# Sixteen-by-sixteen diagonal blocks moved as one strided piece a lane, in a linear-attention and two-layer MLP kernel on one core

## The chip, the cores and the metric

The kernel runs on one core of one Trainium2 chip. The metric is the device time of one execution in microseconds (us); a kernel's time is the median over its runs.

## What is computed

The reference has three parts. The first is a recurrence over 768 positions for 4 x 8 heads, with a 40 x 40 state a head:

```python
for t in range(S):
    y[:, :, t] = np.einsum('bhd,bhde->bhe', rt, state)
    Sa = np.einsum('bhde,bhe->bhd', state, at)
    state_decay = state * wt[:, :, None, :] - np.einsum('bhd,bhe->bhde', Sa, bt)
    state = state_decay + np.einsum('bhd,bhe->bhde', vt, kt)
```

Its output, as 3072 rows of 320, goes through a gated layer (sigmoid(x @ w_gate) * (x @ w_val), 1536 wide, then w_out) and through a second layer (the maximum of three products, 768 wide, then w_out). All is f32.

## The kernel before

**Tiling.** The recurrence is worked in chunks of 64 positions. An "item" is two chunks of four pairs of heads; there are 24 items, in 12 pairs. Inside a chunk the recurrence is a triangular system, so each chunk needs the inverse of a 64 x 64 unit triangle. It is built from 16 x 16 diagonal inverses, which are joined to 32 x 32 (`join`) and to 64 x 64 (`merge`) by small matmuls. The two MLP layers run as f32 products split into high and low parts; their first products (`wave`, L923 to L953) fill TensorE between the small matmuls of the recurrence, and after some 600 us only MLP work is left.

**The way of the diagonal blocks.** For each pair of items `prep` forms the triangles N on VectorE (L438) and writes their 32 x 32 diagonal blocks to the DRAM tensor d1 (L449, eight DMAs). Each 32 x 32 block is one row of 4 KB in d1. `tri` (L479) then does the following.
- Two DMAs (L487) bring the two 16 x 16 diagonal sub-blocks of every 32 x 32 block back, one on each half of the 128 lanes, into the tile T.
- 28 small operations (L497 add, L499 multiply) invert all 128 blocks at once by substitution, on VectorE for the first two pairs and on GpSimd for the other ten; a memset (L505) sets the ones on the diagonal.
- ScalarE copies T transposed into the tile Tt (L506).
- Two DMAs (L510) write Tt into the diagonal places of the DRAM tensor d2, whose other places were set to zero once (L356).

`spread` reads d2 by four DMAs into the tile E (L522), in another arrangement of lanes, and VectorE transposes E (L525). `join` follows (matmuls L543 and L554), then `merge` (L576, L587), `ga` (L605) and the four `step`s that carry the state (L633, L651, L665, L689).

**What sets the order.** Every operation is a task with a duration, reads and writes. A planner (`Plan.play`) plays them through a model of the engines and writes out one fixed order for each engine; the tile framework then puts in the semaphore waits. All data DMAs are issued by SyncE, whose queue SP is in order: a DMA that must wait holds up all that stands behind it. Behind L522 on SP stand the loads of the next items (`ew`, L381 and L382 or L384; 836 KB each) and of `vr` (L624) and `vk` (L627). VectorE and GpSimd are in order too.

**Places.** The tiles share areas of SBUF: T0 and T1 (two slots of T, 128 x 16 x 16) lie in the area F1 (F in the profile), Tt in B3 (B in the profile). The planner also has a rule that could add filler matmuls (`fill`), with its level at 0.0, at which it adds none.

Of the kernel before, what the change touches and what calls it, by code (L numbers as in the profile page):

```python
# [9 lines left out]
BF16 = mybir.dt.bfloat16  # L10
# [5 lines left out]
B, H, S, D = 4, 8, 768, 40  # L16
NTOK, DM = B * S, H * D
C = 64
NP = 4
# [11 lines left out]
            F1=["N0", "N1", "N2", "N3", "DC", "T0", "T1", "Y2"], F2=["MA0", "MA1", "MA2", "MA3", "TD0"],  # L31
            B3=["E0", "E1", "YM0", "Tt", "tmpPOOL"], B4=[f"KH{k}" for k in range(6)],
# [46 lines left out]
class Task:  # L79
    def __init__(self, eng, dur, fn, name):  # L80
        self.eng, self.dur, self.fn, self.name = eng, dur, fn, name
        self.before, self.after, self.users = set(), set(), []
        self.filler, self.fills, self.late = False, 0, 0.0
        self.lat, self.goal, self.due, self.banks, self.keep, self.nbytes = 0.0, 1e9, 1e9, [], None, 0


class Plan:
# [10 lines left out]
    SPARE, AHEAD, MORE = 0.7, 7.0, 1  # L98
    FILL, LEVEL = 0.23, 0.0
    HOLD, BY = 0.4, 40.0  # L100

    def __init__(self):
        self.tasks, self.wrote, self.readers = [], {}, {}
        self.warm = False
        self.stage = None
# [36 lines left out]
    def play(self):  # L142
# [18 lines left out]
        pe_end, done_work = 0.0, []  # L161
# [8 lines left out]
        while len(order) < len(self.tasks):  # L170
            for e, q in ready.items():
# [4 lines left out]
                while q:  # L176
# [5 lines left out]
                    if (t.rank <= hold + self.BY or t.dur < self.HOLD) and all(reader.get(p, (e, 0))[0] == e or reader[p][1] <= now + 1e-9 for p in t.of) and (  # L182
# [5 lines left out]
                        if e == "PE" and t.filler:  # L188
                            self.fill(t, now, pe_end, done_work, clock)
                        if e == "PE":  # L190
                            now_ = now + t.late
                        t.start = now
                        t.end = free_at[e] = clock.run(now_, t.dur, t.name) if e == "PE" else now + t.dur
# [5 lines left out]
                        if e == "PE":  # L199
                            pe_end = t.end  # L200
                            done_work.append((now_, t.end, Clock.WORK.get(t.name, 0.94) * t.dur))
                            credit = credit - t.dur if t.thin else min(self.DENSE, credit + t.dur)
# [33 lines left out]
    def fill(self, t, now, before, work, clock):  # L236


        end = now + t.dur
        lo = end - Clock.TICK  # L240
        while work and work[0][1] < lo - 4 * Clock.TICK:
            work.pop(0)
        got = t.dur * Clock.WORK.get(t.name, 0.94)
        for a, b, w in work:
            if b > lo:
                got += w * (b - max(a, lo)) / (b - a)
        one = self.FILL / (1.0 if clock.warm else 0.51)
        idle = min(self.SPARE * max(0.0, now - before), self.AHEAD)
        n = max(0, math.ceil((self.LEVEL - got) / (0.9 * self.FILL)))
        n = max(min(n, int(idle / one) + self.MORE), int(idle / one) if n else 0)  # L250
        if not n:
            return
        t.fills = n
        at = max(before, now - n * one)
        stop = clock.run(at, n * self.FILL, "fill")
        work.append((at, stop, 0.9 * n * self.FILL))
        t.late = max(0.0, stop - now)

    def emit(self):
        for t in self.play():  # L260
            if t.fills:
                self.filled(t)
            if t.fn:
                t.fn()


class Attn:
# [6 lines left out]
    def open(self, mem, ps):  # L274
# [3 lines left out]
                      ST=[L, NP, D], ew=[L, EWW], AB=[L, NU, C], SW=[L, NP, D], T=[128, 16, 16], Tt=[128, 16, 16], DC=[128, 2 * NU, C], Y2=[128, 2 * NU, 16],  # L278
# [22 lines left out]
        self.pl.filled = self.filled  # L301
# [30 lines left out]
    def pe(self, dur, fn, reads, room, name, keep, n=1):  # L332
        t = self.pl.add("PE", dur, fn, reads, (), name, psum=keep, room=room, n=n)
        t.filler = self.pl.warm and name != "x"
        return t

    def filled(self, t):

        x = self.c.bitcast(BF16)
        for n in range(t.fills):  # L340
            self.nc.tensor.matmul(self.ps[t.banks[0]], x[:, 0:128], x[:, 128:640], start=True, stop=True)


    def begin(self):
# [13 lines left out]
        self.pl.add("POOL", 0.3, lambda: nc.gpsimd.memset(self.tY[0], 0.0), (), ["tY"], "z")  # L358
        for k in range(B):
            for j in range(2):  # L360
                self.pl.add("POOL", 0.18, lambda k=k, j=j: nc.gpsimd.memset(self.SW[k][j], 0.0), (), [("SW", k, j)], "z")
# [117 lines left out]
    def tri(self, i0, slot):  # L479
# [4 lines left out]
        d1 = self.d1[k // 2].rearrange("h t y (a b) -> (h t y) a b", b=32)  # L484
        for h in range(2):
            p, s = slice(64 * h, 64 * h + 64), slice(16 * h, 16 * h + 16)
            self.load(lambda p=p, s=s: nc.sync.dma_start(out=T[p], in_=d1[:, s, s]),  # L487
# [17 lines left out]
        self.pl.add("POOL", 0.15, lambda: nc.gpsimd.memset(T.rearrange("p i j -> p (i j)")[:, 0:256:17], 1.0), (), tT, "one")  # L505
        self.act(570, lambda: nc.scalar.copy(self.Tt, T.rearrange("p i j -> p j i")), tT, ["Tt"], "Tt")  # L506
        q = 32 * (i0 % 4)
        for h in range(2):
            p, s = slice(64 * h, 64 * h + 64), slice(16 * h, 16 * h + 16)
            self.load(lambda p=p, s=s: nc.sync.dma_start(out=self.d2[q:q + 64, s, s], in_=self.Tt[p]), ["Tt", ("d2", k // 2)],  # L510
# [204 lines left out]
    def add(self):  # L715
        self.begin()
        self.pl.warm = True
# [723 lines left out]
```

## Time and profile before

| | us |
|---|---|
| median of 3 runs | 1149.53 |
| lowest and highest run | 1143.75, 1161.09 |
| the profiled execution, its own time | 1145.82 |
| its span, first to last instruction | 1143.9 |
| TensorE matmuls busy | 1057.4 (92% of the span) |
| VectorE, ScalarE, GpSimd busy | 655.4, 498.8, 384.9 |

The profile is one execution. PE is the matmul queue of TensorE, PEld its weight loads, SPq the time that SyncE's queue needs to issue a DMA. A row of the timeline gives the start, the duration, the engine, the line, the tiles and, in brackets, how long the engine had stood idle and what ended that. The chain of waits is followed back from the last instruction, at each step to what released it.

### The profile page before, as it was taken

What the parts mean: (1) busy time and instruction counts of PE and PEld (TensorE: products, weight loads), DVE (VectorE), ACT (ScalarE), POOL (GpSimd) and SP (SyncE); (2) the same over time, 40 slices, a digit from 0 to 9 for tenths busy, and PEclk for the clock granted to TensorE, in tenths of its full rate; (3) what the DMA queues carried; (4) which work ended last, traced back from release to release, by engine and by line L of the source; (5) the groups of instructions that cost most, each with busy time, mean ns of one, the idle gap of its engine ahead of it and who ended that gap; (6) DMA issues with size and microseconds to landing.
All of it is one profiled execution on the core that took longest, in us unless ns stands there. A gap on an engine that the chain in (4) does not pass through costs nothing.

```text
span 1143.9 us, 28812 instructions
## 1 busy us (share of the span) xinstructions
PE 1057.4 (92%) x11954; PEld 887.2 (78%) x11954; DVE 655.4 (57%) x1144; ACT 498.8 (44%) x1091; POOL 384.9 (34%) x551
## 2 busy tenths in 40 slices
PE   5389889999999999998889999999999999999997
PEld 4388677787888787786677778888888888888886
DVE  7679647677668586659873792492493222222122
ACT  2166456576656575667543443353323122122111
POOL 1024523244234344333354553353322222122110
PEclk9995759898978998968879999999999999999999
DMA  6736545475475565554540623333232011000000
GB/s 160 169 97 156 105 94 108 99 168 123 85 170 114 112 151 109 132 160 142 176 152 10 199 71 111 111 107 111 85 117 91 11 51 51 1 33 17 8 23 26
DMA packets 190159, 114.85 MB, mean 100 GB/s; under 512 B 123158, under 2 KB 166806, under 8 KB 188150
## 3 DMA queue, kind: packets, MB, share of 16 engines
q1 hardware_dynamic: 190022, 112.94, 38.5%
q8 instruction: 96, 1.57, 0.6%
q14 instruction: 41, 0.34, 0.1%
HBM read 87.21 MB, written 25.69 MB: 99 GB/s over the span
## 4 chain that ended last, share of the span: by engine, by line
PE 75%; DVE 10%; DMA 5%; issue 4%; ACT 2%; SPq 2%; POOL 1%; DVEq 0%; POOLq 0%; ACTq 0%
PE ps L902 39%; PE ps L972 6%; PE ps L1042 5%; PE ps L605 3%; PE ps L651 3%; PE ps L689 3%; PE ps L665 3%; PE ps L945 3%; DMA D<-ew 2%; PE ps L554 2%; PE ps L633 1%; DMA Q<-ew 1%; PE ps L543 1%; PE ps L468 1%; PE ps L576 1%
## 5 line engine op out<-in xcount | busy, mean ns | idle before, releaser
L748 POOL TENSOR_TENSOR C<-C,C 128x512 fp32r<-128x512 f32 x76 | 102.3, 1347 | 323.4 <-ACT C L911 319.3
L902 PE MATMUL ps<-Q,B 128*128 128x512 f32 x768 | 182.7, 390 | 0.0
L902 PEld LDWEIGHTS ps<-Q,B 128*128 128x128 f32 x768 | 143.0, 188 | 28.5
L911 ACT CAST C<-C 128x512 fp32r<-128x512 f32 x108 | 67.1, 621 | 224.3 <-DVE C L1056 138.5
L1056 DVE TENSOR_TENSOR C<-ps,C 128x512 f32<-128x512 f32 x72 | 49.8, 692 | 189.9 <-PE ps L902 189.9
L902 PE MATMUL ps<-Q,D 128*128 128x512 f32 x480 | 115.7, 393 | 0.0
L902 PE MATMUL ps<-Q,A 128*128 128x512 f32 x384 | 111.6, 444 | 0.0
L925 DVE TENSOR_TENSOR C<-ps,C 128x512 f32<-128x512 f32 x72 | 49.6, 689 | 105.2 <-PE ps L902 100.3
L902 PEld LDWEIGHTS ps<-Q,D 128*128 128x128 f32 x480 | 90.8, 190 | 19.1 <-issue 0.3
L902 PEld LDWEIGHTS ps<-Q,A 128*128 128x128 f32 x384 | 79.1, 213 | 18.8 <-issue 0.6
L902 PE MATMUL ps<-Q,F 128*128 128x512 f32 x384 | 92.2, 389 | 0.0
L707 POOL TENSOR_TENSOR R<-B 104x256 f32<-104x256 f32 x48 | 44.3, 923 | 140.4 <-DVE B L705 138.9
L902 PEld LDWEIGHTS ps<-Q,F 128*128 128x128 f32 x384 | 72.1, 188 | 15.0
L923 ACT ACTIVATE C<-ps 128x512 f32<-128x512 f32 x72 | 42.9, 597 | 81.3 <-PE ps L902 75.8
L499 POOL TENSOR_TENSOR B<-F 128x14 f32<-128x14 f32 (+6 forms) x140 | 47.2, 337 | 76.0 <-DMA F<-d 66.5
L1042 PE MATMUL ps<-R,C 128*128 128x320 f32 x432 | 69.1, 309 | 0.2 <-DVE C L748 0.2
L1042 PEld LDWEIGHTS ps<-R,C 128*128 128x128 f32 x432 | 66.1, 188 | 3.2 <-DVE C L748 0.4
L689 PE MATMUL ps<-Q,B 128*64 128x104 f32 (+1 forms) x768 | 55.7, 288 | 7.8 <-ACT Q L676 3.5
L672 DVE TENSOR_TENSOR Q<-ps,R 64x256 f32<-64x256 f32 x96 | 40.6, 423 | 34.4 <-PE ps L665 24.5
L689 PEld LDWEIGHTS ps<-Q,B 128*64 128x64 f32 (+1 forms) x768 | 43.2, 144 | 18.3 <-DVE Q L672 5.3
L665 PE MATMUL ps<-Q,Q 104*64 104x104 f32 x768 | 54.7, 292 | 1.5 <-ACT Q L654 1.5
L497 POOL TENSOR_TENSOR F<-F,B 128x14 f32<-128x14 f32 (+6 forms) x140 | 51.0, 364 | 10.3
(162 smaller groups left out, 1948.9 us busy)
## 6 DMA issues: line engine op xcount, KB each, us to landing
D<-ew SPq DMA_DIRECT2D x18, 835.7 KB
part<-C SPq DMA_DIRECT2D x30, 256.0 KB
Q<-part SPq DMA_DIRECT2D x30, 256.0 KB
D<-in SPq DMA_DIRECT2D x14, 512.0 KB
Q<-vr SPq DMA_DIRECT2D x32, 208.0 KB
x<-Q SPq DMA_DIRECT2D x18, 256.0 KB
Q<-x SPq DMA_DIRECT2D x18, 256.0 KB
R<-vk SPq DMA_DIRECT2D x48, 80.0 KB
```

Source lines behind the costliest of these rows:

```text
L497: e.tensor_tensor(out=T[:, j + 1:16, 0:j], in0=T[:, j + 1:16, 0:j], in1=t, op=ALU.add)
L499: e.tensor_tensor(out=t, in0=T[:, j + 1:16, j:j + 1].to_broadcast([128, k, j]), in1=T[:, j:j + 1, 0:j].to_broadcast([128, k, j]), op=ALU.mult)
L665: nc.tensor.matmul(ps[64 * x:64 * x + 64, n, 0:L], GA[:, x * NP + n], X[:, x * NP + n], start=True, stop=True)
L689: nc.tensor.matmul(ps[64 * x:64 * x + m, n, 0:L], KH[:, h * D:h * D + m], Z[:, h], start=True, stop=True)
L707: self.pool(256, lambda: nc.gpsimd.tensor_tensor(out=Y, in0=tY, in1=P, op=ALU.mult), ["tY", ("P", i % NB["P"])], [("Y", s % NB["Y"])], "Y")
L748: eng.tensor_tensor(out=out, in0=a, in1=hi.bitcast(F32), op=ALU.subtract)
L902: nc.tensor.matmul(self.bank(t), a[:, c], b, start=n == 0, stop=n == len(ops) - 1)
L911: self.act(NT, lambda: nc.scalar.copy(hi(), h()), [th], [t1], "hi")
L925: self.dve(NT, lambda: nc.vector.tensor_tensor(out=sg(), in0=self.bank(t2), in1=sg(), op=ALU.mult), [tsg], [tsg], "gate", of=t2)
L972: nc.tensor.matmul(self.bank(a, m), u[:, c], v(), start=f == f0 and n == 0, stop=f == 11 and n == 2)
L1042: nc.tensor.matmul(self.bank(a, k)[:, 0:DM], u()[:, c], v, start=f == 0 and n == 0, stop=f == 5 and n == 2)
L1056: self.dve(NT, lambda t=t, h=h: nc.vector.tensor_tensor(out=h(), in0=self.bank(t), in1=h(), op=ALU.max), [th], [th], "max", of=t)
```

## The change

T and Tt become 128 x 16 x 32, so that each lane holds 16 rows with a pitch of 32 elements, as the 32 x 32 blocks in d1 and d2 have. A transfer then takes 496 consecutive elements (1984 B) of a lane, from the first element of a diagonal sub-block to its last, where before it took 16 rows of 16 elements (64 B). Between the rows lie 16 elements that do not belong to the sub-block: coming in, they are what d1 holds there and are not used; going out, they are zeros, for which Tt is set to zero once at the start by a new memset on GpSimd. They fall on places of d2 that are zero. The transfers of a pair stay four, to the same lanes, and L449, L522 and all later steps are as before. T1 moves from the area F1 to B3. The filler rule is taken out of the planner; the order that it writes out holds the same matmuls. In the diff, lines of the new kernel stand 45 or so lower in number.

```diff
-            F1=["N0", "N1", "N2", "N3", "DC", "T0", "T1", "Y2"], F2=["MA0", "MA1", "MA2", "MA3", "TD0"],
-            B3=["E0", "E1", "YM0", "Tt", "tmpPOOL"], B4=[f"KH{k}" for k in range(6)],
+            F1=["N0", "N1", "N2", "N3", "DC", "T0", "Y2"], F2=["MA0", "MA1", "MA2", "MA3", "TD0"],
+            B3=["E0", "E1", "YM0", "Tt", "T1", "tmpPOOL"], B4=[f"KH{k}" for k in range(6)],
...
-    SPARE, AHEAD, MORE = 0.7, 7.0, 1
-    FILL, LEVEL = 0.23, 0.0
...
-T=[128, 16, 16], Tt=[128, 16, 16]
+T=[128, 16, 32], Tt=[128, 16, 32]
...
         self.pl.add("POOL", 0.3, lambda: nc.gpsimd.memset(self.tY[0], 0.0), (), ["tY"], "z")
+        self.pl.add("POOL", 0.3, lambda: nc.gpsimd.memset(self.Tt, 0.0), (), ["Tt"], "z")
...
-        d1 = self.d1[k // 2].rearrange("h t y (a b) -> (h t y) a b", b=32)
+        d1 = self.d1[k // 2].rearrange("h t y a -> (h t y) a")
+        flat, Tt = (x.rearrange("p i j -> p (i j)")[:, 0:496] for x in (T, self.Tt))
         for h in range(2):
-            p, s = slice(64 * h, 64 * h + 64), slice(16 * h, 16 * h + 16)
-            self.load(lambda p=p, s=s: nc.sync.dma_start(out=T[p], in_=d1[:, s, s]),
+            p, s = slice(64 * h, 64 * h + 64), slice(528 * h, 528 * h + 496)
+            self.load(lambda p=p, s=s: nc.sync.dma_start(out=flat[p], in_=d1[:, s]),
...
-        self.pl.add("POOL", 0.15, lambda: nc.gpsimd.memset(T.rearrange("p i j -> p (i j)")[:, 0:256:17], 1.0), (), tT, "one")
-        self.act(570, lambda: nc.scalar.copy(self.Tt, T.rearrange("p i j -> p j i")), tT, ["Tt"], "Tt")
+        self.pl.add("POOL", 0.15, lambda: nc.gpsimd.memset(flat[:, 0:496:33], 1.0), (), tT, "one")
+        self.act(570, lambda: nc.scalar.copy(self.Tt[:, :, 0:16], T[:, :, 0:16].rearrange("p i j -> p j i")), tT, ["Tt"], "Tt")
...
-            p, s = slice(64 * h, 64 * h + 64), slice(16 * h, 16 * h + 16)
-            self.load(lambda p=p, s=s: nc.sync.dma_start(out=self.d2[q:q + 64, s, s], in_=self.Tt[p]), ["Tt", ("d2", k // 2)],
+            p, s = slice(64 * h, 64 * h + 64), slice(528 * h, 528 * h + 496)
+            self.load(lambda p=p, s=s: nc.sync.dma_start(out=self.d2[q:q + 64].rearrange("b i j -> b (i j)")[:, s], in_=Tt[p]), ["Tt", ("d2", k // 2)],
```

SP's queue at the start, from the second block's return (L487, `tri2`) over the first block's way out (L510, `tri0`) to its spread (L522), before:

```order
L624 DMA Q_99<-vr 104x4x128
L624 DMA Q_98<-vr 104x4x128
L487 DMA F_90<-d_57 64x16x16
L510 DMA d_58<-B_92 64x16x16 x2
L487 DMA F_90<-d_57 64x16x16
L627 DMA R_96<-vk 64x320
L522 DMA B_92<-d_58 32x16x32 x4
```

The same place of the changed kernel, where L443, L466 and L478 are the old L487, L510 and L522:

```order
L580 DMA Q_99<-vr 104x4x128
L580 DMA Q_98<-vr 104x4x128
L443 DMA B_92<-d_57 64x496
L466 DMA d_58<-B_92 64x496 x2
L443 DMA B_92<-d_57 64x496
L583 DMA R_96<-vk 64x320
L478 DMA B_92<-d_58 32x16x32 x4
```

No instruction has moved; four transfers have another form, and T1 is now named by the area B. The same holds over the whole queue.

GpSimd's first memsets of tiles, before (B_92 is the area with E, R_95 holds the states, B_94 the tile tY):

```order
L354 MEMSET B_92 128x1024
L361 MEMSET R_95 104x160 x2
L358 MEMSET B_94 104x256
L354 MEMSET B_92 128x1024
L361 MEMSET R_95 104x160 x6
```

The same place of the changed kernel:

```order
L308 MEMSET B_92 128x1024
L313 MEMSET B_92 128x512
L316 MEMSET R_95 104x160 x2
L312 MEMSET B_94 104x256
L308 MEMSET B_92 128x1024
L316 MEMSET R_95 104x160 x6
```

One memset, that of Tt, has come in second, ahead of those of the states. TensorE's, VectorE's and ScalarE's orders hold the same instructions at the same places.

## Rows read from the trace of the kernel before

**Rows 1.** The page: the chain that ended last, by engine.
```profile
PE 75%; DVE 10%; DMA 5%; issue 4%; ACT 2%; SPq 2%; POOL 1%; DVEq 0%; POOLq 0%; ACTq 0%
```

**Rows 2.** Windows: stretch, length, busy of PE, PEld, DVE, ACT, POOL, clock, DMA share, GB/s.
```profile
60.00:540.00 480.00, 446.78 (x8589) 374.91 (x8584) 343.09 (x634) 295.41 (x706) 183.23 (x376) 0.85 0.54 125
540.00:1143.90 603.90, 581.32 (x2842) 487.81 (x2842) 270.62 (x407) 189.41 (x351) 197.75 (x158) 0.97 0.24 75
```

**Rows 3.** Waits: who waited for whom, us in total, times, longest.
```profile
POOL B L499 <- DMA F<-d: 66.5, 10, 13.7
DVE F L525 <- DMA B<-d: 15.9, 5, 8.4
PE ps L543 <- DMA B<-d: 9.2, 4, 7.1
```

**Rows 4.** Issues on SP by line: ns shortest, median and longest.
```profile
L487 SPq DMA_DIRECT2D F<-d x24: 600/661/1302, 24.5 to 466.6; - x24
L510 SPq DMA_DIRECT2D d<-B x24: 601/656/1679, 38.6 to 486.3; - x24
L356 SPq DMA_DIRECT2D d<-B x1: 357/357/357, 6.2 to 6.2; - x1
...
L627 SPq DMA_DIRECT2D R<-vk x48: 484/518/4800, 30.7 to 566.9; - x48
```

**Rows 5.** Timeline 24 to 45 us, the first two blocks.
```profile
38.63 1.64 SPq L510 DMA_DIRECT2D d<-B  x2
40.32 0.67 SPq L487 DMA_DIRECT2D F<-d  x1
...
42.71 1.91 SPq L522 DMA_DIRECT2D B<-d  x4
...
44.79 0.26 PE L543 MATMUL ps<-B,F 32*32 32x16 f32 x2 [7.09 <-DMA B<-d]
```

**Rows 6.** Timeline 387 to 390 us: a load of vk and its reader.
```profile
387.55 0.51 SPq L627 DMA_DIRECT2D R<-vk  x1
...
389.99 0.72 ACT L628 COPY Q<-R 64x640 f32<-64x640 f32 x1 [0.20 <-DMA R<-vk]
```

**Rows 7.** Timeline 128 to 144 us, the third block's way out and the fourth's return.
```profile
128.86 1.36 SPq L510 DMA_DIRECT2D d<-B  x2
130.31 1.98 SPq L487 DMA_DIRECT2D F<-d  x2
132.38 1.39 SPq L624 DMA_DIRECT2D Q<-vr  x1
133.87 2.17 SPq L522 DMA_DIRECT2D B<-d  x4
...
138.42 1.25 DVE L525 STREAM_TRANSPOSE F<-B 128x1024 f32<-128x1024 f32 x1 [1.93 <-DMA B<-d]
```

**Rows 8.** The chain of waits, pieces: start, us, what.
```profile
212.21 3.15 DMA B<-d
...
307.16 3.73 DMA F<-d
318.43 7.02 DMA D<-ew
...
387.01 2.30 DMA B<-d
```

**Rows 9.** Groups by line and form: busy us, mean ns, idle before.
```profile
L499 POOL TENSOR_TENSOR B<-F 128x56 f32<-128x56 f32 x20 | 9.0, 449 | 1.5
...
L497 POOL TENSOR_TENSOR F<-F,B 128x56 f32<-128x56 f32 x20 | 7.9, 396 | 1.4
```

**Rows 10.** Timeline 0 to 11 us: the first memset, the first matmuls.
```profile
0.74 0.95 POOL L354 MEMSET B<- 128x1024 f32 x1 [0.29 <-POOLq L1431]
...
4.53 1.18 PEld L633 LDWEIGHTS ps<-R 104*40 104x40 f32 x8 [4.53 <-POOL R L361]
...
10.99 1.65 PE L468 MATMUL ps<-R,D 104*128 104x104 f32 x8 [4.88 <-DVE D L410]
```

More of the change, by code (lines that the diff above doesn't have):

```diff
@@ L1 @@
-import math
 from contextlib import ExitStack
@@ L9 @@
 F32R = mybir.dt.float32r
-BF16 = mybir.dt.bfloat16
 AF = mybir.ActivationFunctionType
@@ L82, in __init__ @@
         self.before, self.after, self.users = set(), set(), []
-        self.filler, self.fills, self.late = False, 0, 0.0
         self.lat, self.goal, self.due, self.banks, self.keep, self.nbytes = 0.0, 1e9, 1e9, [], None, 0
@@ L103, in __init__ @@
         self.tasks, self.wrote, self.readers = [], {}, {}
-        self.warm = False
         self.stage = None
@@ L160, in play @@
         now, seq, credit = 0.0, 0, self.DENSE
-        pe_end, done_work = 0.0, []
         clock = Clock()
@@ L187, in play @@
                             t.banks, banks[:] = banks[:t.n], banks[t.n:]
[L188 to L191, printed above, removed]
                         t.start = now
-                        t.end = free_at[e] = clock.run(now_, t.dur, t.name) if e == "PE" else now + t.dur
+                        t.end = free_at[e] = clock.run(now, t.dur, t.name) if e == "PE" else now + t.dur
                         done = t.end + max(t.lat, self.LAT[1] * any(b.eng == "PE" for b in t.before))
@@ L199, in play @@
                         if e == "PE":
-                            pe_end = t.end
-                            done_work.append((now_, t.end, Clock.WORK.get(t.name, 0.94) * t.dur))
                             credit = credit - t.dur if t.thin else min(self.DENSE, credit + t.dur)
@@ L234, in play @@
         return order
[L236 to L257, printed above, removed]
     def emit(self):
         for t in self.play():
-            if t.fills:
-                self.filled(t)
             if t.fn:
@@ L277, in open @@
                       GA=[L, 2 * NU, C], XZ=[128, 2, 2 * NP, L], VR=[L, NP, 168], Y=[L, NP, C], tY=[L, NP, C],
-                      ST=[L, NP, D], ew=[L, EWW], AB=[L, NU, C], SW=[L, NP, D], T=[128, 16, 16], Tt=[128, 16, 16], DC=[128, 2 * NU, C], Y2=[128, 2 * NU, 16],
+                      ST=[L, NP, D], ew=[L, EWW], AB=[L, NU, C], SW=[L, NP, D], T=[128, 16, 32], Tt=[128, 16, 32], DC=[128, 2 * NU, C], Y2=[128, 2 * NU, 16],
                       E=[128, 2 * NU, C], TD=[128, 2 * NU, 32], YM=[128, 2 * NU, 32], tmpPOOL=[128, 64],
@@ L333, in pe @@
         t = self.pl.add("PE", dur, fn, reads, (), name, psum=keep, room=room, n=n)
-        t.filler = self.pl.warm and name != "x"
         return t
[L337 to L341, printed above, removed]
     def begin(self):
@@ L716, in add @@
         self.begin()
-        self.pl.warm = True
         for i in range(4):
```

1 line of the change is left out of this document (removed).

## The prediction

> **What bounds the kernel now.** I read the chain by engine first: TensorE holds 75% of it, DMA 5%, SP's issuing 2% [rows 1]. The windows come next. From 540 us to the end only MLP work is left and PE is busy for 581 of 604 us; nothing of the change reaches that far, so what it can win or lose it does before 540. From 60 to 540 us PE is busy for 446.8 of 480 us at a mean granted clock of 0.85, so 33.2 us are idle, and half the full clock was granted for 0.15 x 480 / 0.5 = 144 us of the stretch [rows 2]. Those 33.2 us and the start's idle time are all that shorter waits could give back directly. Third, the waits on the transfers that change. GpSimd waits 66.5 us in total for the returning blocks (F<-d), but it is not the engine the end hangs on. The spread (B<-d) is waited for by the matmuls of L543 for 9.2 us, of which one wait is 7.1 us, and by VectorE's transpose L525 for 15.9 us in five waits [rows 3]. The one of 7.1 us is at the start, where PE stands idle until 44.79 [rows 5]. So the blocks' way through DRAM counts at the start and where VectorE, in order, stands at L525.
>
> **What the change removes.** 48 transfers (24 in, 24 out) each go from 1024 pieces of 64 B to 64 pieces of 1984 B. Each costs two things: the issue on SP and the time to landing. The issue takes 661 ns (L487) and 656 ns (L510) in the median. A transfer of 64 lanes with one piece each stands in the trace: vk, 1280 B a lane, takes 518 ns; L356, one piece of 4 KB on each of 128 lanes, took 357 ns [rows 4]. I take 0.52 us, the nearest row, which saves 0.14 us an issue; the bounds are nothing and 0.30. As to landing, the second L510 of the start's pair begins at 38.63 + 0.71 = 39.34 (half of the 1.64 us is the pair's other issue, with a gap) and L522, which waits for it, begins at 42.71, so 3.37 us from issue to use [rows 5]. The chain has 3.73 us for a returning block [rows 8]. A load of vk is used 389.99 - 387.55 = 2.44 us after its issue began [rows 6]. I take 2.44 us for the new transfers, since it is the nearest row in shape and size; the bounds are 2.44 and 3.37, and a loss only if the bytes count (a rival below).
>
> Here the Trainium skill has a rule that speaks against the change. Its page "DMA: Bandwidth & Descriptors", section "Anatomy of one DMA", fits a DMA as about 2.0 us fixed plus its bytes over 436 GB/s, with no term for the number of pieces; the fit is for the other way of issuing, from GpSimd. By it a transfer of 124 KB in place of 64 KB lands 0.14 us later, not earlier. The rows agree with it as to the fixed part (2.44 us for 80 KB) but not as to the 64 KB transfers, which take 3.4 to 3.7 us.
>
> **The sum, place by place.**
> - The start. L510's pair is issued by SP in 2 x 0.52 + 0.05, the second beginning at about 39.1 instead of 39.34, counting the L487 ahead of it too; it lands by 41.5, so L522 moves from 42.71 to 41.5. SP is free by then, as L487 (40.32) and L627 behind it are also earlier. PE waits for nothing else at 44.79. Gain 1.2 us, bounds 0.4 and 1.5. To the first block's return, further ahead, I give nothing, as ScalarE's copy, which L510 waits for, stands in its queue behind the copies of the first steps; if it counted it would be 3.37 - 2.44 = 0.9 more.
> - 128.86 to 133.87 us. SP runs L510 twice, L487 twice and a load of vr, and reaches L522 with no wait for the landing [rows 7]. The four issues take 3.43 us with gaps; at 0.52 and a gap of 0.05 each they take 2.28. The load of vr behind them took 1.39 us and I give it 0.9, since the four before it leave 256 pieces where 4096 were queued. L522 is then 1.7 us earlier, of which VectorE's wait at L525 can use 1.93 [rows 7]. Gain 1.7, bounds 0.3 and 1.9.
> - The spreads that land in the chain's pieces of 212.21 and 387.01 [rows 8]: there too SP goes from the issues of the blocks to L522 with no wait for a landing, and each saves 0.14, two ahead of the one, four ahead of the other. Gain 0.8 together, bounds 0 and 1.8 (at 0.30 an issue).
> - 307 us: GpSimd gets its block 3.73 us after the second issue, on the chain; at 2.44 that is 1.3 us less. The next piece of the chain is a load of ew issued at 318.43 [rows 8], which is released through GpSimd's work, so it moves along. Gain 1.3, bounds 0 and 1.5.
> - The other seven of the twelve blocks: PE's waits at L543 are but for tenths all at the start, and L525 waits in five places only [rows 3]. Gain 0, hidden by the other work of PE and VectorE; if that cover were gone each would give up to 2 x 0.9 us.
>
> Together 5.0 us less, of 33 + 7 us of idle time that could be had; bounds 0.7 and 6.7 from these places alone.
>
> **What it adds.** One memset of 128 x 512 on GpSimd, half of the 0.95 us that 128 x 1024 took; behind it are the memsets of the states, which PE's first matmuls wait for at 4.53. These move to about 5.0, and PE's next work begins at 10.99 on VectorE's result [rows 10]: hidden, 0, at most 0.5. The 28 small operations and the copy keep their element counts, and only the pitch of their rows doubles. No row shows that pitch; the nearest are two forms of 56 elements, of which one writes packed rows and the other rows of T, 449 and 396 ns [rows 9]. The difference of 53 ns as a bound of either sign makes 29 x 0.053 = 1.5 us a block, which counts in the first two blocks, where VectorE does them: 3 us either way; I take 0, as the form that writes into T is no dearer. 48 x 60 KB = 2.9 MB more are moved, over DMA engines that are busy for 0.54 of the time [rows 2]: 0 here, priced below. No wait is added, and the filler's removal removes no instruction.
>
> The sum for the profiled execution is 1145.8 - 5.0 = 1140.8 us (its span is 1.9 us shorter than its time, and all terms lie inside the span). The median of the three runs is 3.7 us above that execution, and the runs are 17 us apart. A new median should lie between the two bases, 1140.8 and 1144.5; I predict 1143 us.
>
> **Rivals.**
> - Hidden anyway: in the steady part another input is late as soon as the block is earlier (a load of ew, a step of the recurrence, PE itself). For it: PE is 93% busy there; the chain has little DMA. Against: the start has no such cover. It leaves those 1.2 us: 1148 us.
> - The bytes count, slower than before. At 125 GB/s, the rate of the stretch [rows 2], a block's 4 x 60 KB more take 2.0 us of the DMA engines. A load of ew queued behind a block's transfers would land that much later, and VectorE, which waits for it, with it. The chain's piece at 318.43 is such a load [rows 8]; taken for three of the blocks it makes 3 x 2.0 = 6 us, less the 1.2 of the start: 1149.5 + 4.8 = 1154 us. It decides if a lane's piece of 2 KB holds an engine longer than its 16 pieces did; a vk of 80 KB used after 2.44 us speaks against.
> - The clock turns. 144 us of the stretch are at 1.2 GHz [rows 2], and which parts these are hangs on how PE's thin matmuls and gaps fall. If earlier blocks close gaps and a fifth of that time goes to 2.4 GHz, it saves 144 x 0.2 x 0.5 = 14 us: about 1130 us. The same the other way gives 1157 us, slower than before; its point of decision is about 10 us more at 1.2 GHz, which takes the 5 us of the forecast.
> - SP is the real limit: the longest issue of a vk load took 4.8 us against 0.52 [rows 4], and it stood right behind an L510 pair. If the small pieces in the rings were the cause, 4.3 us of SP's time come free there and a like amount in the other long issues. The chain gives SP only 2% [rows 1], so the forecast counts none of it; if two such places counted it would be 1143 - 8.6 = 1134 us.
>
> **Chances.** Forecast 0.42; hidden 0.20; bytes 0.08; clock better 0.10, clock worse 0.10; SP 0.10. Range 1129 to 1158, which takes in both clock cases and the spread of the runs. A change of 2% (23 us) is about what a measurement of this kernel can tell from none: faster than 1126.5 needs the better clock and SP together, 0.07; slower than 1172.5 needs twice the worse clock, 0.03; within, 0.90.
>
> **What would show it.** In the profile of the changed kernel: L443 and L466 issue in about 0.5 us; the first L543 begins near 43.5 us instead of 44.79, and the first waiting GpSimd or VectorE row after a return is 2.4 to 2.9 us behind its issue; L478 after the third block comes 1.7 us sooner behind its L466; VectorE's wait for B<-d falls from 15.9 us to about 11; no SP issue behind an L466 pair takes over 2 us. I am wrong if landings stay at 3.3 us or more, if VectorE's waits for ew grow, or if the granted clock from 60 to 540 us leaves 0.82 to 0.88.

## The result, and the profile after

The changed kernel is on record with 1157.01 us in the median of 20 executions (1144.58 to 1162.92), the kernel before with 1151.88 (1141.38 to 1161.70, also 20). The ratio is 1.0068 with a 95% interval of 1.0039 to 1.0097. This is inside the forecast range and inside 2%, but the kernel looks slower where 5.0 us less, and a median of 1143, were forecast. The ratio, here and in the experiments, is taken from the executions that lie no more than 1.5% above the fastest of their own kernel, which here are 18 of the changed kernel and 13 of the kernel before. The means of those are 1156.1 and 1148.3 us; the means of all 20 and 20 are 1156.8 and 1152.6, a difference of 4.2 +- 3.6 us (as everywhere below, the interval is of 95%). So almost half of the 0.68% comes from which executions are counted: the kernel before has the fastest one (1141.38), and for that its seven longest drop out. The profiled execution of the changed kernel took 1144.58 us (span 1142.7), 1.2 us less than that of the kernel before, not 5.0.

One observation has to come first, since the rest of the ratio can't be read without it. Some executions take about 1146 us and others about 1157, at nearly the same granted clock. For the executions of the kernel before that others are compared with, which it is goes by the place of the execution among the others, as the lists further down show. The profiled execution is mostly one of the shorter ones (16 of the 20 that were taken are under 1150 us). On record 10 of 20 executions of the kernel before were under 1150 us, and one of 20 of the changed kernel, the profiled one. The experiments below look for how much of the difference this makes.

The page of the changed kernel, engines, chain and DMA totals:

```profile
PE 1056.2 (92%) x11954; PEld 886.6 (78%) x11954; DVE 654.9 (57%) x1144; ACT 498.4 (44%) x1091; POOL 389.2 (34%) x552
...
DMA packets 144079, 117.79 MB, mean 103 GB/s; under 512 B 74006, under 2 KB 120726, under 8 KB 142070
...
PE 74%; DVE 10%; DMA 6%; issue 4%; ACT 2%; POOL 1%; SPq 1%; DVEq 0%; POOLq 0%; ACTq 0%
```

The chain differs from [rows 1] by one per cent each in PE, DMA and SP, too little to read from one execution. The DMA totals of the kernel before were these:

```profile
DMA packets 190159, 114.85 MB, mean 100 GB/s; under 512 B 123158, under 2 KB 166806, under 8 KB 188150
```

That is 46080 fewer packets now and 2.9 MB more, which is the change (48 x 960, 48 x 60 KB). The windows of the changed kernel, with the columns of [rows 2]:

```profile
60.00:540.00 480.00, 444.82 (x8572) 373.52 (x8570) 343.24 (x630) 294.86 (x707) 186.78 (x376) 0.86 0.52 131
540.00:1142.70 602.70, 581.35 (x2842) 487.83 (x2842) 269.24 (x405) 189.24 (x351) 198.01 (x158) 0.98 0.24 74
```

PE's busy time, its clock and what follows 540 us are what they were. The DMA engines are busy for 0.52 in place of 0.54 although they move more. The waits that answer to [rows 3], and VectorE's for ew, first the one of the kernel before and then those of the changed kernel:

```profile
DVE D L400 <- DMA D<-ew: 23.9, 11, 5.0
```

```profile
POOL B L455 <- DMA B<-d: 38.8, 5, 10.6
...
POOL B L455 <- DMA F<-d: 22.3, 4, 12.1
DVE D L355 <- DMA D<-ew: 21.1, 14, 4.4
...
DVE F L481 <- DMA B<-d: 13.9, 4, 7.6
...
PE ps L499 <- DMA B<-d: 10.6, 5, 7.0
```

The buffer of T moved, so half of the returns are now named B<-d. VectorE's wait for the spread fell from 15.9 to 13.9 us, its wait for ew from 23.9 to 21.1; PE's did not fall in this execution (9.2 to 10.6). The issues on SP, to be held against [rows 4] (ns shortest, median, longest):

```profile
L443 SPq DMA_DIRECT2D F<-d x12: 481/578/759, 24.4 to 430.6; - x12
L443 SPq DMA_DIRECT2D B<-d x12: 462/568/600, 37.6 to 464.4; - x12
...
L466 SPq DMA_DIRECT2D d<-B x24: 472/584/1394, 38.1 to 484.5; - x24
...
L583 SPq DMA_DIRECT2D R<-vk x48: 470/512/1288, 30.5 to 565.8; - x48
```

The issue of a changed transfer fell by 0.08 us, not by the 0.14 that the forecast took. The longest issue of a vk load fell from 4800 to 1288 ns. The timeline of the start and of the third block, as [rows 5] and [rows 7]:

```profile
38.14 1.22 SPq L466 DMA_DIRECT2D d<-B  x2
39.40 0.60 SPq L443 DMA_DIRECT2D B<-d  x1
...
42.35 1.91 SPq L478 DMA_DIRECT2D B<-d  x4
...
44.33 0.26 PE L499 MATMUL ps<-B,F 32*32 32x16 f32 x2 [6.99 <-DMA B<-d]
...
127.24 1.13 SPq L466 DMA_DIRECT2D d<-B  x2
128.47 1.19 SPq L443 DMA_DIRECT2D B<-d  x2
129.75 2.10 SPq L580 DMA_DIRECT2D Q<-vr  x1
132.70 1.91 SPq L478 DMA_DIRECT2D B<-d  x4
...
136.60 1.25 DVE L481 STREAM_TRANSPOSE F<-B 128x1024 f32<-128x1024 f32 x1 [2.82 <-DMA B<-d]
```

At the start the spread issue comes 0.36 us earlier and PE 0.46; from the second way-out issue (38.14 + 0.61 = 38.75) to L478 it is 3.60 us, more than the 3.37 of before. In the third block the four issues take 2.42 us from the first of L466 to the end of L443, near the forecast (2.28), but the load of vr behind them took 2.10 us where 0.9 was forecast, and L478 came 5.46 us behind its first L466, not 3.3.

### The profile page after: what moved, and what is told of

It is laid out like the page before. It is cut to its first block, busy times and chain, and to the rows that moved or that the text cites. A ratio compares the mean times of both kernels' runs of the same rounds, so it can differ in the third digit from the quotient of the medians.

```text
span 1142.7 us, 28813 instructions
## 1 busy us (share of the span) xinstructions
PE 1056.2 (92%) x11954; PEld 886.6 (78%) x11954; DVE 654.9 (57%) x1144; ACT 498.4 (44%) x1091; POOL 389.2 (34%) x552
## 4 chain that ended last, share of the span: by engine, by line
PE 74%; DVE 10%; DMA 6%; issue 4%; ACT 2%; POOL 1%; SPq 1%; DVEq 0%; POOLq 0%; ACTq 0%
PE ps L857 39%; PE ps L927 6%; PE ps L997 5%; PE ps L561 3%; PE ps L607 3%; PE ps L621 3%; DMA D<-ew 3%; PE ps L900 3%; PE ps L645 3%; PE ps L510 2%; PE ps L423 1%; PE ps L532 1%; PE ps L589 1%; PE ps L929 1%; PE ps L928 1%
## 5 line engine op out<-in xcount | busy, mean ns | idle before, releaser
L857 PEld LDWEIGHTS ps<-Q,A 128*128 128x128 f32 x384 | 78.3, 211 | 18.4 <-issue 0.6
L621 PEld LDWEIGHTS ps<-Q,Q 104*64 104x64 f32 x768 | 45.6, 164 | 11.0 <-issue 6.7
L703 POOL TENSOR_TENSOR Q<-Q,Q 128x512 fp32r<-128x512 f32 x33 | 46.0, 1411 | 18.2 <-ACT Q L842 18.2
```

The costliest lines, as they stand in the source:

```text
L621: nc.tensor.matmul(ps[64 * x:64 * x + 64, n, 0:L], GA[:, x * NP + n], X[:, x * NP + n], start=True, stop=True)
L703: eng.tensor_tensor(out=out, in0=a, in1=hi.bitcast(F32), op=ALU.subtract)
L857: nc.tensor.matmul(self.bank(t), a[:, c], b, start=n == 0, stop=n == len(ops) - 1)
```

## The experiments

Each run has 12 executions of its own, and its ratio is to executions of the kernel before that were taken in the same set (35 of them, or 17 where a kernel stands alone). Kernels of one set ran on the same chip. For each run the mean of all 12 executions is given too, since the two lengths of execution make a median jump. Such a mean is known to some 3.5 us. The changed kernel is the base of all edits.

**First set: both kernels, and the transfers put back.** The first run, e1_before, is the kernel before without an edit, and e2_after the changed kernel without an edit. e3_layout puts both transfers back to sixteen rows of 64 B and keeps all else of the change:

```diff
+        dn = self.d1[k // 2].rearrange("h t y (a b) -> (h t y) a b", b=32)
...
-            self.load(lambda p=p, s=s: nc.sync.dma_start(out=flat[p], in_=d1[:, s]),
+            self.load(lambda p=p, s=s: nc.sync.dma_start(out=T[p][:, :, 0:16], in_=dn[:, (s.start // 528) * 16:(s.start // 528) * 16 + 16, (s.start // 528) * 16:(s.start // 528) * 16 + 16]),
...
-            self.load(lambda p=p, s=s: nc.sync.dma_start(out=self.d2[q:q + 64].rearrange("b i j -> b (i j)")[:, s], in_=Tt[p]), ["Tt", ("d2", k // 2)],
+            self.load(lambda p=p, s=s: nc.sync.dma_start(out=self.d2[q:q + 64, 16 * (s.start // 528):16 * (s.start // 528) + 16, 16 * (s.start // 528):16 * (s.start // 528) + 16], in_=self.Tt[p][:, :, 0:16]), ["Tt", ("d2", k // 2)],
```

Here `s.start // 528` is the half, 0 or 1.

e4_in does only the second of these two replacements, so that the way in stays in one piece and the way out is in rows.

e1_before. 

> The kernel before against itself, for the spread of the comparison and for the trace of another execution. All theories: ratio 1.000, interval no wider than 0.6% to each side. If executions differ by some ten us from one to the next in one place (theory M: the program has several courses, and a change only shifts how often each is taken), this trace and that of the next run, laid beside those in hand, show the place: one stretch of 20 to 100 us in which the distance of like matmuls grows by 8 us or more.

e2_after. 

> The changed kernel again. If the +0.7% is real, ratio 1.004 to 1.010. Theory M: its profiled execution is one of 1152 to 1160 us, and its distance from the execution of 1144.6 us comes about in one or two places before 600 us. Theory of the bytes: the distance grows by about 2 us at each block, most where VectorE waits for ew.

e3_layout. 

> Undoes both transfer forms (16 rows of 64 B in and out) and keeps all the rest: T and Tt with rows 32 apart, T1 in the area B3, the memset of Tt, no filler rule. If the wide transfers cost the time (bytes): ratio 1.000 (0.997 to 1.003). If the layout does (pitch of the small operations, T1 in B3, the memset): ratio 1.004 to 1.010, and the small operations on GpSimd are dearer than before.

e4_in. 

> Blocks come back in one piece of 1984 B a lane, and go out in 16 rows of 64 B; the rest as in the changed kernel. Bytes: about half of the loss, 1.002 to 1.005. Layout: the whole, 1.004 to 1.010, as in the run with both forms undone. The forecast's mechanism alone: 0.998, by the landing that is earlier at the start and at 307 us.

Measured: e1_before 0.9964 [0.9922, 1.0006], mean 1153.2 us; e2_after 0.9901 [0.9864, 0.9938], 1148.0; e3_layout 0.9957 [0.9907, 1.0007], 1155.7; e4_in 0.9955 [0.9918, 0.9992], 1151.8. The changed kernel is here faster than the kernel before, where 1.004 to 1.010 was expected if the loss on record were real, and the kernel before held against itself is off by 0.4%. So a ratio of one set is not to be trusted to half a per cent. Of the four means only those of the changed kernel and of layout alone lie clearly apart (by 7.7 +- 5.9 us). Layout alone, with wider rows and the memset, is no faster than the kernel before.

**Second set: none, one and two of each transfer.** e5_before and e6_after are the two kernels without an edit. e7_none leaves out all 48 transfers of the diagonal blocks (the returning block and the inverse), so d2 keeps its zeros and the output is not the reference's; T is set to zero once by two more memsets:

```diff
-            self.load(lambda p=p, s=s: nc.sync.dma_start(out=flat[p], in_=d1[:, s]),
+            self.load(None,
...
-            self.load(lambda p=p, s=s: nc.sync.dma_start(out=self.d2[q:q + 64].rearrange("b i j -> b (i j)")[:, s], in_=Tt[p]), ["Tt", ("d2", k // 2)],
+            self.load(None, ["Tt", ("d2", k // 2)],
```

e8_twice issues each of the 48 a second time, the return to a tile that nobody reads (1280 B a lane), the inverse to a DRAM tensor that nobody reads (1984 B a lane):

```diff
-            self.load(lambda p=p, s=s: nc.sync.dma_start(out=flat[p], in_=d1[:, s]),
+            self.load(lambda p=p, s=s: (nc.sync.dma_start(out=flat[p], in_=d1[:, s]), nc.sync.dma_start(out=self.twin[p], in_=d1[:, s.start:s.start + 320])),
...
-            self.load(lambda p=p, s=s: nc.sync.dma_start(out=self.d2[q:q + 64].rearrange("b i j -> b (i j)")[:, s], in_=Tt[p]), ["Tt", ("d2", k // 2)],
+            self.load(lambda p=p, s=s: (nc.sync.dma_start(out=self.d2[q:q + 64].rearrange("b i j -> b (i j)")[:, s], in_=Tt[p]), nc.sync.dma_start(out=self.d3[q:q + 64].rearrange("b i j -> b (i j)")[:, s], in_=Tt[p])), ["Tt", ("d2", k // 2)],
```

e5_before. 

> The kernel before again, as a run of its own beside the changed kernel in one set of runs. On record stands a ratio of 1.0068; the second set gave 0.9901 for the changed kernel and 0.9964 for the kernel before against itself. Theory of the spread (each set draws other executions, and the interval of one set is too narrow): 0.995 to 1.005. If the own runs of a kernel are always lower than those of the kernel they are compared with: about 0.996 again.

e6_after. 

> The changed kernel a third time. Theory of the spread: within 0.99 to 1.007 of the kernel before, and within 0.6% of the run of the kernel before in the same set. Theory of a real loss (bytes or layout): slower than the run of the kernel before in the same set by 0.4% or more. The forecast's mechanism, 5 us: faster by 0.4%.

e7_none. 

> Leaves out all 48 transfers of the blocks (T stays at zero but for ones on the diagonal, d2 stays zero); all else is issued in the same order, so nothing waits for a block any more. It bounds what any cheaper transfer can give. Forecast's sum: at least its 5 us, and up to 15 (ratio 0.987 to 0.996 against the kernel before). Hidden anyway: 2 to 3 us at the start at most, ratio 0.997 or more. Bytes: faster than the changed kernel by 6 us or more.

e8_twice. 

> The changed kernel with every one of the 48 transfers issued a second time, to places that nothing reads (1280 B a lane for those that come back, 1984 B for those that go out): twice the SP issues, 1.8 times the bytes. Bytes: 6 us or more above the changed kernel. SP as the limit: 48 x 0.58 = 28 us of SP's time more, of which a tenth to a third shows, 3 to 9 us. Hidden anyway: within 2 us of the changed kernel but for the start.

Measured: e5_before 0.9960 [0.9917, 1.0002], mean 1154.1 us; e6_after 0.9952 [0.9918, 0.9987], 1149.6; e7_none 0.9918 [0.9882, 0.9954], 1145.7; e8_twice 0.9989 [0.9947, 1.0032], 1159.3. By the means, taking the transfers away altogether is worth 8.5 +- 5.2 us against the kernel before and 3.9 +- 4.1 against the changed one, and a second copy of each costs 9.7 +- 5.9. So the transfers are on the path in part, and even the best form of them could win no more than about 8.5 us. Some of that may be the clock: the mean granted clock of the 12 executions is 0.931 without the transfers, 0.926 in e5_before and 0.929 in e6_after, and a line through the 72 executions of either kernel that were run without an edit gives 3.8 and 5.5 us less for each 0.01 more. The timeline of PE at the first spread matmul, in e6_after, e7_none and e8_twice in this order:

```profile
44.40 0.26 PE L499 MATMUL ps<-B,F 32*32 32x16 f32 x2 [6.42 <-DMA B<-d]
```

```profile
43.10 0.25 PE L501 MATMUL ps<-B,F 32*32 32x16 f32 x2 [4.54 <-DMA B<-d]
```

```profile
46.30 0.26 PE L499 MATMUL ps<-B,F 32*32 32x16 f32 x2 [8.30 <-DMA B<-d]
```

Even without the diagonal transfers 4.54 us of PE's wait remain, and with two of each it is 8.30. VectorE's waits for ew and for the spread move the same way; of e7_none and then of e8_twice:

```profile
DVE D L357 <- DMA D<-ew: 13.3, 9, 2.2
...
DVE F L483 <- DMA B<-d: 9.4, 4, 3.7
```

```profile
DVE D L355 <- DMA D<-ew: 21.5, 10, 5.0
...
DVE F L481 <- DMA B<-d: 16.0, 5, 5.2
```

In e6_after these two are 17.8 and 11.1 us. The windows from 60 to 540 us of e7_none and e8_twice show where the rest goes:

```profile
60.00:540.00 480.00, 442.45 (x8607) 372.89 (x8602) 353.33 (x643) 299.35 (x717) 187.75 (x378) 0.89 0.48 122
```

```profile
60.00:540.00 480.00, 448.54 (x8612) 377.12 (x8606) 341.77 (x628) 291.88 (x701) 179.65 (x371) 0.85 0.56 138
```

The kernel without them gets its work through earlier (643 VectorE instructions done by 540 us in place of 628) at a clock of 0.89 against 0.85. Both are single executions; over all 12 the mean granted clock of the two is 0.931 and 0.928.

**Third set: the other half, and the order turned.** e9_after now runs ahead of e10_before; both are without an edit. e11_out makes only the first replacement of e3_layout (the way in is in rows again, the way out in one piece); e12_layout is e3_layout once more.

e9_after. 

> The changed kernel, fourth time, first of its set. Spread: a mean between 1146 and 1158 us, and lower or higher than the kernel before by chance; forecast's mechanism at its measured size (0.5 us a landing, 0.08 us an issue): with the 24 own runs so far of each, 1148.8 against 1153.6 us, the mean of the kernel before in the same set lies 2 to 5 us above.

e10_before. 

> The kernel before, after the changed one in the same set. Spread: 1150 to 1158 us. A real loss as on record would put it 5 us or more below the run of the changed kernel.

e11_out. 

> Blocks go out in one piece of 1984 B a lane and come back in 16 rows of 64 B; the rest as in the changed kernel. Forecast's mechanism: the way out is the one that PE and VectorE wait for (start, third block), so most of the gain, 1 to 4 us below the run with both forms undone (mean 1155.7). In the trace: the first spread's matmuls at 44 to 44.5 us, an issue of the way out in 0.585 us, of the way back in 0.66.

e12_layout. 

> Both forms undone and the new layout kept, second time. Spread alone: 1150 to 1158 us. If the layout costs at the start what its first trace showed (first spread's matmuls at 45.6 against 44.9 us), that shows again, 45.3 us or later, and the mean is 0 to 2 us above the kernel before.

Measured: e9_after 0.9950 [0.9909, 0.9991], mean 1151.7 us; e10_before 0.9975 [0.9935, 1.0016], 1154.2; e11_out 0.9914 [0.9873, 0.9955], 1151.0; e12_layout 0.9969 [0.9930, 1.0009], 1152.8. In time, the two halves alone (e4_in 1151.8, e11_out 1151.0) can't be told from layout alone (1155.7 and 1152.8) nor from the changed kernel (1148.0 to 1151.7); which half carries more is below what 12 executions tell. The waits of the traces do tell. The first spread matmul and the issues of vk of e11_out, where only the way out is in one piece, and then of e4_in, where only the way in is:

```profile
44.41 0.26 PE L500 MATMUL ps<-B,F 32*32 32x16 f32 x2 [6.77 <-DMA B<-d]
...
L584 SPq DMA_DIRECT2D R<-vk x48: 484/510/1214, 30.8 to 565.8; - x48
```

```profile
45.54 0.26 PE L499 MATMUL ps<-B,F 32*32 32x16 f32 x2 [7.26 <-DMA B<-d]
...
L583 SPq DMA_DIRECT2D R<-vk x48: 470/512/4632, 31.2 to 563.8; - x48
```

Layout alone has 45.62 and 45.79 us for that matmul, and 4732 and 4905 ns for the longest issue of vk. Summed over the 12 blocks, the time from the first way-out issue to the spread issue is 56.1 us in e11_out and 64.7 in e4_in, against 65.4 with layout alone. So the way out is the half that shortens the path to the spread and the long issue of vk; that was expected of e11_out, though a gain of it in time is not shown.

**Each kernel alone with the kernel before.** No edit in either; each is one kernel beside the kernel before, as on record.

e13_after_alone. 

> The changed kernel as the only kernel compared with the kernel before, as in the result on record. If the arrangement made the +0.68% (the same program runs higher or lower by where it stands among the others): above 1.002. If the result on record was a draw from the spread, or that chip's own: 0.990 to 0.998, as in the three sets with other kernels.

e14_before_alone. 

> The kernel before alone against itself. Arrangement: above 1.002, by as much as the run of the changed kernel alone is above its 0.9934 of the three sets. Otherwise 0.996 to 1.000, as three times before.

Measured: e13_after_alone 1.0018 [0.9980, 1.0056], mean 1154.4 us; e14_before_alone 1.0032 [0.9988, 1.0075], 1156.0. Taken alone, the unchanged kernel comes out 0.7% higher against itself than it did in the first two sets, as expected if the arrangement decides, and no lower than the changed one (1.0018, just short of the 1.002 that this theory asked for). By the means, the unchanged kernel is 4.3 +- 4.1 us above the executions that it is compared with, as much as the changed kernel on record (4.2). Of its own executions 1 of 12 is under 1150 us here, and 2 of 12 of the changed kernel, as 1 of 20 on record; in the other sets it is 22 and 28 of 60. The executions of the kernel before in these two sets, as they are listed, in us:

```
with e13: 1142 1157 1163 1148 1156 1158 1153 1157 1147 1156 1158 1144 1153 1147 1158 1146 1159
with e14: 1144 1157 1158 1145 1159 1155 1154 1159 1146 1156 1158 1142 1152 1145 1152 1143 1156
```

In both the places 1, 4, 9, 12, 14 and 16 are the short ones (mean 1145.9 and 1144.1) and all others are long (1157.1 and 1155.9), on two chips. In the first three sets of four, places 1, 5 and 9 of the 35 are short (1147.6, 1146.7 and 1146.1 in the mean) and the median of the others is 1158; one of the others, in the first set, took 4353 us. The granted clock of short and long places differs by 0.003 to 0.005 in these two sets, which at that rate is 1 to 3 us. In the first set of four it is 0.927 in both, and in no set do they differ by more than 0.008; so the clock makes a small part of the 11 us at most.

**Last set: the two kernels in the order before, changed, changed, before.** No edit in any.

e15_before. 

> The kernel before, unchanged, first of four (order: before, changed, changed, before). Theory (the change gains 2 to 5 us, and the 0.68% on record is the place of the executions in their order): the mean of this run and of e18 lies 2 to 5 us above that of e16 and e17, and the ratio of this unchanged kernel to the comparison kernel is off 1 by 0.3 to 0.5%. Rival (the change costs 0.68%, as on record): this run and e18 lie 4 to 8 us below e16 and e17.

e16_after. 

> The changed kernel, unchanged, second of four. Theory: about 1150 us in the mean, 2 to 5 us under the mean of e15 and e18. Rival: 1158 us or more, above both.

e17_after. 

> The changed kernel once more, third of four. Theory: within 3 us of e16 in the mean, 2 to 5 us under e15 and e18. If e16 and e17 differ by more than 4 us, the place in the set decides more than the kernel, and the sign stays open. Rival: 1158 us or more.

e18_before. 

> The kernel before once more, last of four. Theory: within 3 us of e15 in the mean, about 1154 us. Rival: about 1150 us, under e16 and e17.

Measured: e15_before 0.9997 [0.9961, 1.0034], mean 1154.8 us; e16_after 0.9972 [0.9933, 1.0010], 1152.1; e17_after 0.9922 [0.9881, 0.9962], 1149.9; e18_before 0.9967 [0.9934, 1.0000], 1151.1. The means of the two pairs are 1153.0 and 1151.0, a gain of 2.0 +- 3.5 us. The rival, a loss of 4 to 8 us, is excluded in this set; the theory's gain of 2 to 5 just fits, though this set alone can't tell it from none. e15 and e18, one kernel, differ by 3.7 us, more than the 3 expected. The comparison kernel's short executions stand again at places 1, 5 and 9 (1145.7 in the mean, the others' median 1156.8).

**All together.** The changed kernel's own executions in the five sets (6 x 12 = 72) have a mean of 1150.9 us, the copies of the kernel before (72) 1153.9: a difference of -3.0 us, with a 95% interval of -5.0 to -1.0, if executions are taken as independent. By set it is -5.1, -4.6, -2.6, -1.7 (e13 and e14, on two chips) and -2.0, of one sign in either order of the kernels. With the 20 and 20 on record taken in it is -1.4 +- 1.8, so a gain is shown by the five sets and not beyond them. It is also no larger than what place alone does: in the sets of four, the copies of the kernel before have means some 3 to 4 us below the same kernel as the one compared with.

## Why the prediction was right or wrong

**The direction on record.** The step that failed is the last one of the sum, "A new median should lie between the two bases, 1140.8 and 1144.5". It laid the 5.0 us on two bases that it took for the level at which the changed kernel would be measured. Both rest on short executions: on the profiled one of 1145.8, and on 1149.53, the middle of two short ones and a long one (1143.75, 1149.53, 1161.09). Measured alone beside the kernel before, a kernel has its own executions mostly among the long ones: 1 of 20 under 1150 us on record, 1 of 12 for the unchanged kernel in e14. So the median came to 1157.0, while the executions of the same changed kernel in the five sets have a mean of 1150.9.

That the recorded +0.68% is a loss through the change is not borne out. Almost half of it comes from which executions are counted; the 4.2 us that are left are no more than the unchanged kernel showed against itself in e14 (4.3 +- 4.1); and the five sets give a gain of 0.26%. That places make the difference between executions is shown for the kernel before by the lists. That they make all of the sign on record is worked out from e14 and the lists and was not shown by itself: the changed kernel alone, in e13, came out 1.2 +- 4.3 us above.

What it is in a place that costs 11 us is open: no trace of a 1157 us execution was taken, as the profile is taken of the first. The four longest executions that were traced without an edit (spans of 1148.8 to 1151.3 us) show where their extra time arises. The 8500th of their 11954 matmuls starts at 503.0 to 504.8 us, that of the ten others at 496.2 to 499.6, and from there to the start of the last it is 637 to 640 us in all 14. So they lose it in the recurrence, ahead of some 500 us.

**The size.** Forecast 5.0 us, measured 3.0 +- 2.0 in the sets. The mechanism, earlier landings and shorter issues at the start and ahead of L478, is seen in the traces; its largest terms were sized too high. The seven traced executions of either kernel differ by only 0.3 +- 3.5 us in their mean span, so the traces tell which waits became shorter, not how much of that the end gained. The means that follow are over these seven traces each, where no other count is given.

- Issues: forecast 0.14 us less each, measured 0.08 (661 and 656 to between 568 and 584 ns). vk at 1280 B a lane was the nearest row; the issues at 1984 B a lane took some 0.06 us more.
- Landing: taken as 2.44 us in place of 3.37, so 0.9 us less. The traces also record, by its semaphore, when the completions of each transfer came. From the start of its issue to its last completion the way out took 3.43 us in the median before and 3.04 after, the return 3.56 and 3.13 (168 transfers each): 0.4 us less. The row was a short one of its kind: the loads of vk themselves have a median of 2.7 us. From the second way-out issue to the spread issue at the start it is 3.52 us before (3.3 to 3.7) and 3.05 after (2.8 to 3.6). Over all 12 blocks the time from the first way-out issue to the spread issue fell from 63.8 to 57.5 us, 0.5 us a block; with layout alone it was 65.4 (two traces). The rule of the Trainium skill that stood against the change (page "DMA: Bandwidth & Descriptors", section "Anatomy of one DMA"), by whose fit the larger transfer lands an estimated 0.14 us later, goes the wrong way here.
- The start: forecast 1.2 us. PE's wait at the first spread matmul fell from 7.23 to 6.49 us, and its start from 45.00 to 43.95. So the start came 1.05 us earlier and the wait fell by 0.7, both within the bounds of 0.4 and 1.5. Of the 1.05, 0.55 lie between the first way-out issue and the spread's; the rest is mainly that the way out began 0.5 us earlier, which its scatter (36.8 to 39.4 us) does not tell from none.
- The third block: forecast 1.7 us, measured 0.3: from the first way-out issue to the spread's it is 4.39 us before and 4.10 after (3.5 to 5.5). The forecast had SP reach L522 "with no wait for the landing". In the trace that it read, the second way-out transfer had landed 0.5 us before; but in five of the six other traces of the kernel before, and in all seven of the changed one, L522 or L478 begins 0.05 us after that landing. So the landing sets this place, not SP's issues, and only the landing's few tenths could be won. The 5.0 us of [rows 7] was the longest of the seven. The load of vr, from which 0.5 us was expected, took 0.85 or 0.86 us in five of the seven traces on either side, so its 1.39 in [rows 7] was one long case. It took 2.10 us in the recorded execution of the changed kernel and 0.86 in e2_after, behind the same four issues, whose timeline is:

```profile
126.66 1.14 SPq L466 DMA_DIRECT2D d<-B  x2
127.89 1.19 SPq L443 DMA_DIRECT2D B<-d  x2
129.18 0.86 SPq L580 DMA_DIRECT2D Q<-vr  x1
130.29 2.52 SPq L478 DMA_DIRECT2D B<-d  x4
...
134.81 1.25 DVE L481 STREAM_TRANSPOSE F<-B 128x1024 f32<-128x1024 f32 x1 [0.51 <-DMA B<-d]
```

- The block at 307 us: forecast 1.3 us, not seen. From the second return issue to GpSimd's first operation on the block it is 3.8 us in the mean before (3.4 to 4.1) and 3.8 after (3.2 to 4.4). In the chain of the changed kernel it has 4.19:

```profile
210.46 3.74 DMA B<-d
...
304.62 4.19 DMA B<-d
317.15 10.95 DMA D<-ew
```

The load of ew behind it is the second of a pair here, and the first of it in [rows 8] (7.02 us). Each of the two loads took nearly the same time in both recorded executions (7.02 and 10.77 us from issue to landing before, 7.05 and 10.95 after).

- The spreads at 212 and 387 (0.8 forecast): there SP does go to L522 without a wait for the landing, as the forecast had it, and from the first way-out issue to the spread's it is 4.65 and 4.62 us before and 4.64 and 4.37 after, so 0.0 and 0.25 less. (The chain's piece at 212 is 3.15 us before and 3.74 after.)
- VectorE's wait for the spread as a whole fell from 14.3 to 11.5 us in the mean (forecast 15.9 to about 11). That is near the forecast size, but the third block, which was to give most of it, did not; over which places it is spread was not followed.
- A term that was not in the sum: VectorE's wait for ew fell from 21.0 to 17.4 us. All seven traces of the kernel before have 18.4 us or more, five of the seven of the changed one less. The bytes rival asked for the opposite. Why it fell was not tested; layout alone has 26.6 and 24.5.
- The small operations, priced at 3 us either way and taken as 0: right. Those on VectorE take 198 ns in the mean with either pitch; those on GpSimd 351 to 363 ns before and 358 to 364 after (three traces each).
- The added memset is hidden as forecast: it took 0.53 us, and PE's first weight load came at 4.30 where it had been 4.53.

```profile
1.63 0.53 POOL L313 MEMSET B<- 128x512 f32 x1
...
4.30 1.18 PEld L589 LDWEIGHTS ps<-R 104*40 104x40 f32 x8 [4.30 <-POOL R L316]
```

- The wider rows of T cost no time that these runs show: layout alone has a mean of 1154.2 us over 24 executions, the kernel before 1153.9 over 72, a difference of 0.3 +- 3.2. At the start they may cost some 0.7 us: the first spread matmul comes at 45.62 and 45.79 us with layout alone, as e12_layout was expected to show again, and at 44.10 to 45.62 in the kernel before.

**The rivals.** Bytes: falls, as the waits for ew and the DMA share (0.54 to 0.52) went down with more bytes, and the 126 loads of ew of 8228 B a lane landed 8.5 us after their issue in the mean before and 8.4 after. That further transfers of this size cost is shown by e8_twice, though this adds issues on SP as well as bytes, and the two were not taken apart. Clock: the mean clock from 60 to 540 us was 0.85 to 0.86 in both recorded profiles, and over the 72 executions of either kernel the mean is 0.928 before and 0.929 after, worth about half a microsecond of the 3.0; more is not shown. SP: in part. The 48 issues took 36.6 us in the mean before and 29.6 after, so 7 us of SP came free, and the long vk issues with them (4732 ns again in e3_layout); but the time did not fall by the 8.6 us of that rival. Hidden anyway: its 1.2 us is inside the interval of the difference, near its lower end, so it can't be ruled out as the size; the waits that fell away from the start, and the 8.5 +- 5.2 us of e7_none where 2 to 3 were asked, speak for more. Of the three signs that the forecast named for being wrong, longer waits for ew and a clock outside 0.82 to 0.88 did not come. Landings of 3.3 us or more came in part: the medians fell below that, but the way out at the start of the recorded execution (3.6) and the return at 307 us (3.8) did not.

## What to carry to other kernels

Forecast a change of under 1% against executions that stand in the same places of a measurement as those it will be held against, and run the unchanged kernel against itself once: here it was off by up to 0.4%, more than the whole effect. Look also at how many executions of each kernel a ratio counts. A term read from one occurrence in one trace (the third block, the load of vk) should be read from several blocks or executions first, as the one that catches the eye is likely a long or a short one, and at each place it should be asked whether the issue or the landing ends last. Here, turning many small pieces into one a lane gave 0.4 us of landing and 0.08 us of issue a transfer; to find what such an edit can win at most, leave the transfers out and, for the slope, issue them twice.

## What the runs showed that was not expected

- In the executions of the kernel before that others are compared with, the place of an execution shifts its time by 11 to 12 us (1145 against 1157), at a granted clock that is the same within 0.008.
- Moving 2.9 MB more in 46080 fewer packets lowered the busy share of the DMA engines, from 0.54 to 0.52 between 60 and 540 us.
- The longest issue of another load on SP (vk, unchanged) was 4112 to 4932 ns in all seven traces of the kernel before and 568 to 1532 in all seven of the changed one. The issues of vk in e3_layout, where the small pieces are back, and in e8_twice, which has twice as many of the large ones:

```profile
L584 SPq DMA_DIRECT2D R<-vk x48: 484/518/4732, 31.3 to 568.0; - x48
```

```profile
L583 SPq DMA_DIRECT2D R<-vk x48: 470/498/1316, 31.1 to 571.6; - x48
```

It was 4732 ns with the small pieces back, and 1316 with double the large ones: the long issue goes with the small pieces, not with the number of transfers. With e4_in (4632) and e11_out (1214), shown above, it goes with those of the way out; in the recorded trace of the kernel before and in e4_in it stands right behind two of them. That these 4 us were worth little of the time agrees with SP's 2% of the chain [rows 1].
